# A fused spectral filter and gated FFN on one core: one weight load on another queue, and the first slabs' steps in another order

## The chip, the cores and the metric

The kernel runs on one core of one Trainium2 chip. The metric is the device time of one execution in microseconds; the time of a kernel is the median of its runs.

## What is computed

The input `x` is 2048 rows of 640 values. Each row is normalized; the normalized rows go two ways. One way is a spectral filter (a two-dimensional real Fourier transform, a product with complex weights, and the inverse transform), computed as matrix products with tables of sines. The other is a gated FFN with 1536 hidden columns. The two meet in the last line.

```python
xn = _layernorm(x, axis=-1)
s = irfft2(rfft2(xn) * (w_r + 1j * w_i)).astype(bfloat16)
h = gelu(xn @ w_gate) * (xn @ w_up)
g = silu(h @ w_down)
return x + s * g
```

## The kernel before

The rows are taken as 16 slabs of 128 rows (`n1` is the slab's number), and X holds them all in the on-chip memory. Four slabs make an FFN group of 512 rows. The hidden columns are 12 tiles of 128. For a group, each tile takes five products with the gate weights Wg (the 640 columns are five chunks of 128) and five with the up weights Wu. ScalarE turns the gate result into its gelu (tile `ge`, L805), and VectorE multiplies it by the up result into `uT` (L807). The products need the normalized rows transposed, `xnT`. For group 0 TensorE itself transposes, chunk by chunk, into a PSUM tile `pt`, and VectorE or ScalarE copies that to `xnT`. Later groups are transposed by DMA.

A slab is normalized in these steps: VectorE takes the statistics of two halves (`bn_half`, L180) and joins them (`bn_join`, L186); the reciprocal root is taken by ScalarE for slab 0 (`root_act`, L205) and by VectorE and GpSimd for the others (`root`: `ve` at L196, the power at L198); VectorE then subtracts and scales in place (`norm`, L209).

The order of all work is written out by hand. Each engine executes its instructions in the order in which the program names them, with semaphores for what it needs from others. `back` is the list of TensorE's FFN steps, and `put(s, ...)` places other work behind step `s`. The steps at the start are these:

- Before step 0: the loads (all on SP's queue), constants, statistics of slabs 0 and 1, warm-up products that feed nothing (`warm_pe`, L600), the normalization and transposes of slab 0 in two parts (`norm_parts`, `slab_Tparts`), the rest of slab 1's statistics and its root, and small constants (`inv_consts`, L261) on VectorE.
- Step 0: the gate products of tiles 0 and 1 for slab 0 (`GG`), slab 1's normalization, slab 0's up products of tile 0, slab 1's transposes, slab 0's up products of tile 1 (`UU`).
- Step 1: gate and up products of tiles 0 and 1 for slab 1; then slab 2's statistics.
- Steps 2 to 7: tiles 2 to 7 for the first half of the group (slabs 0 and 1, 256 columns). Behind them slab 2 is normalized (step 2) and transposed (step 4), slab 3 normalized (step 5) and transposed (step 6).
- Steps 8 to 15: tiles 0 to 7 for the second half (slabs 2 and 3). From step 16 on, tiles take 512 columns at once.

Weights come in pieces of two tiles (`load_w`, `load_gu`): each piece has 128 rows in five runs of 512 bytes, 320 KB. Slabs 0 to 3 are loaded one by one, 160 KB each, in rows of 1280 bytes.

The filter's stages lie between the later FFN steps and are not touched.

Of the kernel before, what the change touches and what calls it, by code (L numbers as in the profile page):

```python
# [32 lines left out]
def kernel(  # L33
# [40 lines left out]
    with tc.manual_schedule():  # L74
        build(nc, locals())


def build(nc, env):
    consts, big, wts, xg, work, psA, psB = (env[k] for k in ("consts", "big", "wts", "xg", "work", "psA", "psB"))
    ZDR, UDR, X, Wg, Wu, Wd, W1, W2 = (env[k] for k in ("ZDR", "UDR", "X", "Wg", "Wu", "Wd", "W1", "W2"))  # L80
    xv, outv, wgv, wuv = (env[k] for k in ("xv", "outv", "wgv", "wuv"))
    A_w_r, A_w_i, B_w_down = (env[k] for k in ("A_w_r", "A_w_i", "B_w_down"))

    def load_x(n0, n, eng=nc.sync):
        eng.dma_start(out=X[:, n0:n0 + n, :], in_=xv[:, n0:n0 + n, :])

    def load_w(k, t0, t1):
        f0, f1 = t0 * P, t1 * P
        nc.sync.dma_start(out=(Wg, Wu)[k][:, :, f0:f1], in_=(wgv, wuv)[k][:, :, f0:f1])

    def load_gu(t0, t1):
        for k in range(2):
            load_w(k, t0, t1)

    load_x(0, 1)
    load_x(1, 1)
    load_gu(0, 2)
    load_gu(2, 4)
    load_x(2, 1)
    load_gu(4, 6)  # L100
# [76 lines left out]
    def bn_half(n1, k):  # L177
        if k == 0:
            st_n[n1] = work.tile([P, 2, nc.vector.BN_STATS_DIM], FP32, tag="st", bufs=3, name="st")
        nc.vector.bn_stats(out=st_n[n1][:, k, :], in_=X[:, n1, 320 * k:320 * k + 320])  # L180

    def bn_join(n1):
        g = n1 // 4
        if g not in mva:
            mva[g] = work.tile([P, 4, nc.vector.BN_AGGR_DIM], FP32, tag="mva", bufs=2, name=f"mva{g}")
        nc.vector.bn_aggr(out=mva[g][:, n1 % 4, :], in_=st_n[n1])  # L186
# [6 lines left out]
    def root(n0, n):  # L193
        m = mva[n0 // 4][:, n0 % 4:n0 % 4 + n, :]
        ve = work.tile([P, 4], FP32, tag="ve", name="ve")[:, 0:n]
        nc.vector.tensor_scalar(out=ve, in0=m[:, :, 1], scalar1=1e-5, scalar2=None, op0=ALU.add)  # L196
        r = work.tile([P, 4], FP32, tag="rst", bufs=4, name="rst")[:, 0:n]
        nc.gpsimd.tensor_tensor(out=r, in0=ve, in1=mhalf[:, 0:n], op=ALU.pow)  # L198
        rall[n0] = r
        for k in range(n):  # L200
            rstd[n0 + k] = r[:, k:k + 1]
# [6 lines left out]
    def norm(n1, c0=0, c1_=D):  # L208
        nc.vector.tensor_scalar(out=X[:, n1, c0:c1_], in0=X[:, n1, c0:c1_], scalar1=mva[n1 // 4][:, n1 % 4, 0:1],  # L209
                                scalar2=rstd[n1], op0=ALU.subtract, op1=ALU.mult)  # L210
        if c1_ == D:
            done.add(("n", n1))
# [46 lines left out]
    def affine(name, src, a, b):  # L259
        t = c1(name)  # L260
        nc.vector.tensor_scalar(out=t, in0=src, scalar1=float(a), scalar2=float(b), op0=ALU.mult, op1=ALU.add)  # L261
        return t
# [43 lines left out]
    def inv_consts(part):  # L306
        if part == 0:
            for k, c in enumerate((0.0, 4.0, 2.0)):
                inv_src[k] = affine(f"i_{k}", pf, 4.0, c)
            kc.append(affine("hk", h_f, -2.0, 1.0))  # L310
        else:
            o = [affine(f"o_{k}", pf, 2.0, c) for k, c in enumerate((320.0, 2.0, 321.0, 1.0))]
            i_0, i_1, i_2 = (inv_src[k] for k in range(3))
            ab.extend([(i_0, o[0]), (i_1, o[1]), (i_2, o[2]), (i_2, o[3])])
# [281 lines left out]
    def warm_pe(n):  # L596
        if not warm_bank:
            warm_bank.append(bank(0))
        for _ in range(n):
            nc.tensor.matmul(warm_bank[0][:, 0:256], lhsT=ones[:, 0:P], rhs=ones, start=True, stop=True)  # L600
# [182 lines left out]
    def bank(k):  # L783
        return psA.tile([P, 512], FP32, tag="gu"[k], name="ps" + "gu"[k])
# [58 lines left out]
    GG, UU = ((0, 0), (1, 0)), ((0, 1), (1, 1))  # L843
# [2 lines left out]
        for it in items:  # L846
            it[0](*it[1:])

    PARTS = (((0, 3), (3, 5)), ((0, 2), (2, 5)))

    def norm_parts(n1):
        for a, b in PARTS[n1]:
            norm(n1, a * P, b * P)

    def slab_Tparts(n1):
        if n1 == 0:
            xnT[0] = xg.tile([P, 5, 512], BF16, tag="xg", name="xnT0")
        evs = (nc.scalar.copy, nc.vector.tensor_copy)
        for (a, b), ev in zip(PARTS[n1], evs[::-1] if n1 == 0 else evs):
            pt = psB.tile([P, 5, P], BF16, tag="b")  # L860
            for c in range(a, b):
                nc.tensor.transpose(out=pt[:, c, :], in_=X[:, n1, c * P:(c + 1) * P], identity=ident)
            ev(out=xnT[0][:, a:b, n1 * P:n1 * P + P], in_=pt[:, a:b, :])
        done.add(("T", n1))

    NP = 8
    back = [(run, (ffn_slab, 0, GG), (norm_parts, 1), (vt_iota, 1), (ffn_slab, 0, UU[:1]), (slab_Tparts, 1),
             (ffn_slab, 0, UU[1:])),
            (run, (ffn_slab, 1, GG + UU), (stats, 2), (root, 2, 1))]
    for h in range(2):  # L870
        for t in range(0 if h else 2, NP):
            back.append((ffn_part, 0, t, h))
    for g in range(4):
        for t in range(NP if g == 0 else 0, NT):
            for k in range(2):
                back.append((ffn_half, g, t, k))
        for j in range(4):
            for q in range(3):
                back.append((down_third, g, j, q))
    plan = [[] for _ in back]  # L880

    def put(s, *item):
        plan[s].append(item)
# [6 lines left out]
    put(4, root, 3, 1)  # L890
    put(4, slab_T, 2, 1)
    put(5, norm, 3)
    put(6, slab_T, 3, 0)
    for g in range(5):
        put(3 + g, ft_v, g)
        put(8 + g, ft_v, 5 + g)
# [79 lines left out]
    for i, (n0, n) in enumerate(DG):  # L976
        a = vs0 + 7 * i
# [12 lines left out]

    warm_pe(18)
    norm_parts(0)
    bn_half(1, 1)
    slab_Tparts(0)
    warm_pe(2)
    bn_join(1)
    root(1, 1)
    inv_consts(0)
    inv_consts(1)

    put(5, phase_const)

# [35 lines left out]
```

## Time and profile before

| | |
|---|---|
| median of 3 runs | 200.24 us (199.80 to 200.43) |
| profiled execution | 199.91 us, of which the profile's span is 198.0 us |
| TensorE busy | 192.3 us, 97% of the span |
| VectorE, ScalarE, GpSimd busy | 131.1, 124.0, 39.8 us |
| gate and up products (L801) | 60.5 and 60.6 us |
| down products (L826) | 30.5 and 28.9 us |
| moved by DMA | 32.43 MB, mean 164 GB/s |

Times in the profile are microseconds from the span's start. PE is TensorE (PEld its weight loads), DVE is VectorE, ACT is ScalarE, POOL is GpSimd, and SPq is the queue from which SP issues transfers. In a row of the timeline the first number is the start and the second the duration, then engine, source line and operation, output and input tiles, shape and count; a bracket gives the idle time ahead of it and what ended that. A row that stands for several instructions reaches from the start of the first to the end of the last, and ends of matmuls overlap the next start. The chain of waits is followed back from the last instruction to whatever released each step, and is listed here in order of time.

### The profile page before, as it was taken

How to read it: one execution, taken by the hardware profiler on the slowest of the kernel's cores; microseconds unless marked ns; L12 is line 12 of the kernel's file. 1: busy time of each engine (PE TensorE's matmuls, PEld its weight loads, DVE VectorE, ACT ScalarE, POOL GpSimd, SP SyncE). 2: the span in 40 equal slices, each digit the busy share in tenths (PEclk: the TensorE clock that was granted, in tenths of full speed). 3: DMA queues.
4: the chain of work that ended last, by engine and by line, in shares of the span. 5: the costliest groups of instructions: out<-in, count | busy, mean ns of one | idle time of the engine just before them, and what ended most of it. 6: DMA issues, size and time to landing. Idle time of an engine off the chain costs nothing.

```text
span 198.0 us, 4139 instructions
## 1 busy us (share of the span) xinstructions
PE 192.3 (97%) x1523; PEld 118.7 (60%) x1538; DVE 131.1 (66%) x314; ACT 124.0 (63%) x218; POOL 39.8 (20%) x68
## 2 busy tenths in 40 slices
PE   7999999999999999999999999999999999999993
PEld 5798854777555555676534343457765555556773
DVE  7787889979899831224666555333349786878673
ACT  4566657876976666634878687524474748376632
POOL 4448679997220110000000000000000000000000
PEclk9999999999999999999999999999999999999998
DMA  5999999657576783329962022439900416042612
GB/s 151 306 328 363 368 319 187 134 145 268 135 193 111 149 311 100 106 69 310 271 180 103 16 86 100 135 98 273 293 4 33 137 37 195 33 136 42 195 62 71
DMA packets 39508, 32.43 MB, mean 164 GB/s; under 512 B 13248, under 2 KB 38464, under 8 KB 39232
## 3 DMA queue, kind: packets, MB, share of 16 engines
q1 hardware_dynamic: 39392, 30.86, 55.4%
q0 software_dynamic: 96, 1.31, 1.7%
q8 instruction: 12, 0.20, 0.5%
q14 instruction: 8, 0.07, 0.1%
HBM read 19.03 MB, written 7.88 MB: 136 GB/s over the span
## 4 chain that ended last, share of the span: by engine, by line
PE 93%; DVE 3%; DMA 1%; issue 1%; ACT 1%; POOL 0%; ACTq 0%
PE psu L801 25%; PE psg L801 25%; PE psg L826 14%; PE psu L826 13%; PE pv L718 2%; PE pd L563 2%; PE pu L663 2%; PE pz L553 2%; PE pd L584 2%; PE px L636 2%; DMA X<-in_A_x_dram 1%; PE pd L567 1%; DVE st L180 1%; DVE X L209 1%; PE pd L586 1%
## 5 line engine op out<-in xcount | busy, mean ns | idle before, releaser
L801 PE MATMUL psg<-xnT,Wg 128*128 128x512 bf16 (+2 forms) x282 | 60.5, 341 | 0.7 <-issue 0.2
L801 PE MATMUL psu<-xnT,Wu 128*128 128x512 bf16 (+2 forms) x283 | 60.6, 342 | 0.4 <-issue 0.2
L807 DVE TENSOR_TENSOR uT<-psu,ge 128x512 bf16<-128x512 f32 (+2 forms) x58 | 34.4, 593 | 25.8 <-PE psu L801 22.9
L826 PEld LDWEIGHTS <-uT 128*128 128x128 bf16 x396 | 37.2, 98 | 14.1 <-issue 0.4
L805 ACT ACTIVATE ge<-psg 128x512 bf16<-128x512 f32 (+2 forms) x58 | 30.4, 523 | 23.1 <-PE psg L801 22.4
L801 PEld LDWEIGHTS <-Wu 128*128 128x128 bf16 x290 | 26.8, 98 | 23.8 <-issue 2.2
L801 PEld LDWEIGHTS <-Wg 128*128 128x128 bf16 x290 | 26.5, 98 | 20.8 <-issue 1.9
L826 PE MATMUL psg<-Wd,uT 128*128 128x320 bf16 (+1 forms) x204 | 30.5, 295 | 0.0
L826 PE MATMUL psu<-Wd,uT 128*128 128x320 bf16 (+1 forms) x192 | 28.9, 296 | 0.0
L648 DVE TENSOR_TENSOR X<-xs,W 128x972 bf16<-128x972 bf16 (+2 forms) x22 | 13.3, 648 | 10.2 <-ACT xs L644 9.2
L589 ACT CAST zd<-pd 128x660 bf16<-128x660 f32 x16 | 11.3, 706 | 10.0 <-PE pd L586 8.4
L180 DVE BATCH_NORM_STATS2 st<-X 128x6 f32<-128x320 bf16 x32 | 14.0, 475 | 0.3 <-DMA X<-in_A_x_dram 0.3
L720 ACT CAST W<-pv 128x640 bf16<-128x640 f32 x16 | 11.1, 696 | 5.0 <-PE pv L718 5.0
L743 ACT ACTIVATE W<-pd 128x960 bf16<-128x960 f32 (+2 forms) x14 | 10.1, 780 | 5.6 <-PE pd L567 5.5
L669 ACT CAST X<-pu 128x486 bf16<-128x486 f32 (+4 forms) x22 | 12.3, 558 | 0.3
L644 ACT CAST xs<-px 128x972 bf16<-128x972 f32 (+2 forms) x11 | 10.3, 937 | 2.9 <-PE px L636 2.9
L835 DVE SCALAR_TENSOR_TENSOR G<-th,psg 128x320 bf16<-128x320 f32 x8 | 3.9, 487 | 12.1 <-ACT th L834 12.1
L555 ACT CAST GEN<-pz 128x640 bf16<-128x640 f32 x16 | 11.2, 699 | 0.0
L749 DVE TENSOR_TENSOR W<-W 128x960 bf16<-128x960 bf16 (+1 forms) x12 | 6.9, 599 | 3.9 <-ACT W L743 3.8
L776 DVE TENSOR_TENSOR Yall<-Yall,G 128x640 bf16<-128x640 bf16 (+3 forms) x19 | 8.2, 434 | 1.6 <-ACT G L831 1.3
L777 DVE TENSOR_TENSOR Yall<-Yall,xt 128x640 bf16<-128x640 bf16 (+3 forms) x19 | 8.3, 439 | 0.7
L198 POOL TENSOR_TENSOR rst<-ve,mhalf 128x1 f32<-128x1 f32 (+1 forms) x6 | 5.4, 902 | 12.8 <-DVE ve L196 12.8
(144 smaller groups left out, 210.9 us busy)
## 6 DMA issues: line engine op xcount, KB each, us to landing
ZDR<-zd SPq DMA_DIRECT2D x32, 80.2 KB, 2.5
UDR<-X SPq DMA_DIRECT2D x10, 240.8 KB, 2.4
xt<-in_A_x_dram SPq DMA_DIRECT2D x14, 160.0 KB, 3.4
out_dram<-Yall SPq DMA_DIRECT2D x14, 160.0 KB, 1.9
B<-ZDR SPq DMA_DIRECT2D x8, 240.8 KB, 4.2
W<-UDR SPq DMA_DIRECT2D x4, 481.5 KB, 6.8
X<-in_A_x_dram SPq DMA_DIRECT2D x3, 640.0 KB, 10.2
Wd<-in_B_w_down_dram SPq DMA_DIRECT2D x1, 1920.0 KB, 14.6
```

The costliest lines, as they stand in the source:

```text
L180: nc.vector.bn_stats(out=st_n[n1][:, k, :], in_=X[:, n1, 320 * k:320 * k + 320])
L555: nc.scalar.copy(out=Zt[n1], in_=pz)
L589: nc.scalar.copy(out=zd.rearrange("p c (q e) -> p c q e", e=10), in_=pd[:, :, 0:330].rearrange("p c (e q) -> p c q e", q=33))
L644: nc.scalar.copy(out=xs, in_=px[:, :, 0:n * w].rearrange("p k (h l) -> p k h l", l=w))
L648: nc.vector.tensor_tensor(out=pp[-1], in0=xs, in1=WT[:, :, h0:h0 + n, l0:l0 + w], op=ALU.mult)
L669: nc.scalar.copy(out=us[:, :, :, c0:c0 + (w + 1 - m) // 2], in_=pv[:, :, :, m:w:2])
L720: nc.scalar.copy(out=vs, in_=pv)
L743: nc.scalar.activation(out=eo[:, b, :, a0:a1].rearrange("p k a n -> p a k n"), in_=py[b][:, a0:a1], func=ACT.Copy, scale=(2.0 if silu[a0] ...
L801: nc.tensor.matmul(ps, lhsT=WT[:, c, t * P:(t + 1) * P], rhs=xnT[g][:, c, c0:c1_], start=(c == 0), stop=(c == 4))
L805: nc.scalar.activation(out=ges[t], in_=ps, func=ACT.Gelu_apprx_tanh)
L807: nc.vector.tensor_tensor(out=uT[g][:, t, c0:c1_], in0=ps, in1=ges[t], op=ALU.mult)
L826: nc.tensor.matmul(ph, lhsT=uT[g][:, t, j * P:(j + 1) * P], rhs=Wd[:, t, c0:c1_], start=(t == 0), stop=(t == NT - 1))
```

## The change

The up weights of tiles 0 and 1 are issued from ScalarE's queue instead of SP's, as its first instruction. On VectorE, slab 1's join and root come ahead of the copy of slab 0's transposes. In step 0, slab 1's transposes come ahead of all of slab 0's up products. Slab 1 is split like slab 0 (three chunks, then two; VectorE copies the three and ScalarE the two). The second part of `inv_consts` moves behind slab 0's up products. Slab 3's transposes move from behind step 6 into step 7, between its gate and its up products, and are split in two parts as well. There is one warm-up product more behind slab 0's transposes.

```diff
-    def load_w(k, t0, t1):
+    def load_w(k, t0, t1, eng=nc.sync):
         f0, f1 = t0 * P, t1 * P
-        nc.sync.dma_start(out=(Wg, Wu)[k][:, :, f0:f1], in_=(wgv, wuv)[k][:, :, f0:f1])
+        eng.dma_start(out=(Wg, Wu)[k][:, :, f0:f1], in_=(wgv, wuv)[k][:, :, f0:f1])
...
     load_x(0, 1)
     load_x(1, 1)
-    load_gu(0, 2)
+    load_w(0, 0, 2)
+    load_w(1, 0, 2, nc.scalar)
     load_gu(2, 4)
...
-    PARTS = (((0, 3), (3, 5)), ((0, 2), (2, 5)))
+    PARTS = ((0, 3), (3, 5))
...
-        evs = (nc.scalar.copy, nc.vector.tensor_copy)
-        for (a, b), ev in zip(PARTS[n1], evs[::-1] if n1 == 0 else evs):
+        for (a, b), ev in zip(PARTS, (nc.vector.tensor_copy, nc.scalar.copy)):
...
-    back = [(run, (ffn_slab, 0, GG), (norm_parts, 1), (vt_iota, 1), (ffn_slab, 0, UU[:1]), (slab_Tparts, 1),
-             (ffn_slab, 0, UU[1:])),
+    back = [(run, (ffn_slab, 0, GG), (norm_parts, 1), (vt_iota, 1), (slab_Tparts, 1), (ffn_slab, 0, UU),
+             (inv_consts, 1)),
...
+        if h == 0:
+            back[-1] = (run, (ffn_piece, 0, NP - 1, 0, 0, 256), (slab_Tparts, 3), (ffn_piece, 0, NP - 1, 1, 0, 256))
...
-    put(6, slab_T, 3, 0)
...
     warm_pe(18)
     norm_parts(0)
     bn_half(1, 1)
-    slab_Tparts(0)
-    warm_pe(2)
     bn_join(1)
     root(1, 1)
+    slab_Tparts(0)
+    warm_pe(3)
     inv_consts(0)
-    inv_consts(1)
```

## The prediction

> **What bounds the kernel now.** I read the page first, then the chain that ended last in order of time, then the timeline and the rates of the first 20 us, where the edits lie.
>
> The chain's shares by engine, on the page:
>
> ```profile
> PE 93%; DVE 3%; DMA 1%; issue 1%; ACT 1%; POOL 0%; ACTq 0%
> ```
>
> TensorE sets the end. Read in order of time, the chain leaves TensorE only in the first 16 us and in the last one; between, it holds nothing but matmuls and gaps of 0.02 to 0.16 us. So a product that starts 0.1 us earlier at 9 or 16 us moves the end by 0.1 us, and nothing later absorbs it. The chain around slab 1:
>
> ```profile
> 5.28 0.40 DVE st L180
> 5.68 0.30 DVE xnT L863
> 5.98 0.13 DVE mva L186
> ...
> 6.13 0.17 DVE ve L196
> ...
> 6.37 0.59 POOL rst L198
> ...
> 6.98 0.36 DVE X L209
> ...
> 7.39 0.29 PE pt L862 x2
> ...
> 8.05 0.37 DVE xnT L863
> ...
> 8.46 0.61 PE psg L801 x8
> 9.07 0.56 PE psu L801 x10
> ```
>
> The copy of slab 0 (5.68) stands inside slab 1's way from statistics to transposes, and TensorE takes up slab 1's gate products fully only at 8.46. The last row gives 0.056 us for a 128-column product. The second place is slab 3, in the timeline:
>
> ```profile
> 14.66 0.71 PE L801 MATMUL psu<-xnT,Wu 128*128 128x256 bf16 x5
> 14.95 0.43 DVE L209 TENSOR_SCALAR X<-X,mva,rst 128x640 bf16<-128x640 bf16 x1
> ...
> 15.44 0.28 PEld L541 LDWEIGHTS <-X 128*128 128x128 bf16 x5 [0.36 <-DVE X L209]
> 15.45 0.45 PE L541 MATMUL pt<-ident,X 128*128 128x128 bf16 x5
> ```
>
> A group of five 256-column products takes 0.54 (the next rows start 0.54 or 0.55 apart), so TensorE was free at 15.20 and began the transposes at 15.45: 0.25 us lost to slab 3's normalization, done at 15.38.
>
> The loads at the start, in the same view:
>
> ```profile
> 0.72 1.28 ACT L221 ACT_TABLE_LOAD   x1 [0.72 <-PEq L1022]
> 0.72 0.86 SPq L85 DMA_DIRECT2D X<-in_A_x_dram  x2
> ...
> 1.64 0.43 SPq L89 DMA_DIRECT2D Wg<-in_B_w_gate_dram  x1
> ...
> 2.10 0.53 SPq L89 DMA_DIRECT2D Wu<-in_B_w_up_dram  x1
> ...
> 4.32 0.29 ACT L205 ACTIVATE rst<-mva,eps 128x1 f32<-128x1 f32 x1 [2.10 <-DVE mva L186]
> ```
>
> The chain begins with slab 0's load, 0.72 to 3.13. Today nothing else moves beside it but slab 1.
>
> **Slab 1 ahead.** Without the copy, the aggregation starts at 5.68 + 0.02. Its whole length is 0.21 (0.08 of that ran under the copy), then 0.02, ve 0.17, 0.07, the power on GpSimd 0.59, 0.03: slab 1's normalization starts at 6.79, not 6.98, a gain of 0.19. The copy (0.36) follows ve, 6.02 to 6.38, and the four inv_consts(0) instructions (0.33 in all) end about 6.65; both lie under the power on GpSimd. The price is slab 0's gate products: their first starts at 6.42 instead of 6.04, ten end at 6.98, before the transposes can start. Today ScalarE's half of that copy ends at 6.38 anyway, so only about 0.1 us of it would show, and TensorE idles then. The third warm-up product (0.11 to 0.21) lies in the same idle time.
>
> The normalization now takes 384 columns first: 0.38 (slab 0's row: 0.64 for both parts, as here), plus 0.05, so three transposes start at 7.22; the other two at 6.79 + 0.64 + 0.05 = 7.48. The ten up products of slab 0 start at 7.59 and end at 8.15. VectorE's copy is ready at 7.22 + 0.36 + 0.37 = 7.95, ScalarE's (0.32 after 7.48, plus 0.37) at 8.17, wanted by the fourth gate product at 8.32. So slab 1's gate runs 8.15 to 8.71 without a stop, and its up products start at 8.71 against 8.91: **0.20 us gained**. The five up products that today fill TensorE's wait ahead of the transposes come behind them; that takes back most of what the wait loses, and is why the gain is not larger. The four inv_consts(1) instructions (0.33) move behind slab 0's up products on VectorE, queued ahead of slab 1's; there VectorE idled 0.76 before 9.46. Cost nothing; were that cover gone, at most 0.33 on VectorE, which TensorE would see only at slab 2's transposes (normalization done 12.38, wanted 12.63).
>
> **Slab 3 in tile 7.** The transposes come one gate group later, at 15.74 on today's clock, 0.36 after the normalization ends. The stall of 0.25 goes: **0.25 us gained**. What is late next are the copies, which keep one up group (0.54) as cover instead of two. VectorE: three transposes from 15.74, copy from 16.12 (behind tile 6's product, 15.47 to 15.89) to 16.48, wanted at 16.57. ScalarE: gelu of tile 7 from 15.94 to 16.32, copy to 16.67, wanted by the fourth product at 16.90. Margins 0.09 and 0.23; a miss costs itself, at most the 0.25.
>
> **The up load from ScalarE's queue.** Its issue (0.53, from SP's row) goes ahead of the table load and warm-up; these then end near 2.75, and ScalarE idled 2.10 before 4.32. Nothing, unless the issue exceeded 2.1 us. On SP every later issue moves up by up to 0.57. The real cost is at the DMA engines:
>
> ```profile
> 2.00:3.00 1.00, 1.00 (x6) 0.74 (x5) 0.77 (x11) 0.20 (x2) 0.13 (x1) 1.00 0.80 285
> 3.00:4.00 1.00, 1.00 (x7) 0.69 (x6) 0.85 (x2) 0.00 (x0) 0.89 (x1) 1.00 0.61 174
> ...
> 5.00:6.00 1.00, 1.00 (x8) 0.74 (x8) 1.00 (x5) 0.99 (x2) 0.00 (x0) 1.00 1.10 314
> ```
>
> (The last two columns are DMA share and GB/s.) The up load now leaves at 0.72 beside slab 0. Its 328 KB at 300 GB/s are 1.09 us, slab 0's 164 KB are 0.55. If all of it goes first, slab 0 is 1.09 late; with equal shares, 0.55; if slab 0's bytes are on the engines first, 0. No row shows two such queues together. I take 0.25, the nearer half: the smaller load also has the shorter issue (0.43 against 0.53), so it should reach the engines no later. The whole chain from 3.13 shifts by that: **0.25 us lost**. The dip at 3 to 4 us (some 0.12 MB) is filled, so the loads behind come up to 0.4 us earlier; this matters only as cover: the up weights of tiles 6 and 7 land at 8.43 + 6.0 = 14.4 and are wanted at 14.55, a margin that the earlier TensorE would else eat. Slab 1's load (1.17 + 2.4 = 3.57) has until 4.20; 0.63 of delay is free.
>
> The Trainium skill, "DMA: Bandwidth & Descriptors", section "Queues, rings and completion order", speaks against this edit: each engine takes turns between queues by packets of about 9 to 17 descriptors. An estimate from it: one such packet of 512-byte rows on 16 engines is 74 to 139 KB, or 0.25 to 0.46 us ahead of slab 0; by its upper end the sum below would be 0.01 above the time before.
>
> **Sum.** -0.20 - 0.25 + 0.25 = -0.20 us. The profiled execution took 199.91 (span 198.0 and 1.91 around it), which is 0.33 below the median 200.24; it becomes 199.71, and the median 200.04.
>
> **Rivals.**
> 1. Slab 0's load is not held at all: -0.45, 199.79. For it: its issue is first on SP and short. Against: both queues start at 0.72.
> 2. Slower: the up load holds slab 0. It decides from 0.45 us of delay on; with equal shares the time is 200.34, with all of its bytes first 200.88. For it: the chain starts with that load and has no slack. Against: slab 0's rows are few, and equal turns by row favour it (1280 bytes against 512). The skill's turns by packets, above, would stop it at 0.46 us of delay and 200.25.
> 3. The TensorE clock rises later. The warm-up shows 4.02 us for 18 products of 256 columns, 0.22 each, and later groups 0.11: in the records the rate doubles between slab 0's transposes (0.107 apart) and its gate products (0.055 apart), near 5.7. The granted-clock column reads 1.00 throughout and does not show it. If it doubled only after slab 1, products at 0.107 put slab 1's up products at 9.86 in the old order and 10.16 in the new one, which has 25 products and transposes between slab 1's normalization and that point where the old has 20. Then +0.30 in place of -0.20, in all 200.54. The new kernel's later start gives TensorE a slightly longer pause before it, which speaks a little for it. The skill's "TensorE: Matmul & The Clock Gate", section "What's actually happening", says the window that decides runs freely, not from the kernel's start; by that the moment varies between executions of either kernel.
> 4. The change does less than it says: the copies of slab 3 miss their cover and the 0.25 comes back: 200.29.
>
> **Chances.** Forecast 0.52, rival 1 0.20, rival 2 0.17, rival 3 0.07, rival 4 0.04. A measurement of this kernel can tell about 0.3%, 0.60 us, from no change (the three runs spread over 0.63). The sum's best case is 0.45, so faster by more needs something that I don't see as well: 0.12, from rival 1. Slower by more needs nearly the whole up load ahead of slab 0, or rivals 2 and 3 together: 0.14. The range runs from rival 1 with half of the runs' spread (199.79 - 0.3) to rival 2's far end: 199.5 to 200.88.
>
> **What would show it.** Slab 0's load in the chain: landing by 3.13 + 0.25 (3.13: rival 1; 3.7 or later: rival 2). Relative to that landing, slab 1's normalization should start 3.66 after it (3.85 today) and its up products 5.58 (5.78 today). The wait of 0.36 at slab 3's transposes should be gone, and tile 0's second half should follow tile 7's up group without a gap. I am wrong if the statistics of slab 0 start on time and the time still doesn't fall, if slab 0's gate products wait for weights beyond 6.98 plus the shift, or if a new wait stands after 17 us.

## The result and the profile after

The changed kernel takes 201.16 us in the median of 22 runs (200.29 to 202.99), the kernel before 199.97 us in as many (199.80 to 201.10). The ratio is 1.0049, 95% interval 1.0031 to 1.0067: slower by half a per cent, above the range of the prediction.

The 22 runs fall into two groups. Ten lie between 200.29 and 200.66 us, twelve between 201.11 and 202.99. So there are two losses: about 0.5 us that every execution has, and one of 0.65 us or more that about half of them have. The profiled execution (202.09 us) has both. Its page begins with the span (198.0 before); part 3 shows the up load as a queue of its own:

```profile
span 200.3 us, 4157 instructions
...
q10 hardware_dynamic: 656, 0.33, 0.6%
```

The chain of waits in order of time (start, duration, what):

```profile
1.17 4.10 DMA X<-in_A_x_dram
...
5.30 0.49 DVE st L181
5.79 0.53 DVE X L210 x2
...
7.24 0.59 POOL rst L199
...
7.86 0.39 DVE X L210
...
8.29 0.69 PE pt L862 x5
8.98 1.07 PE psu L802 x10
10.05 1.07 PE psg L802 x10
```

The chain no longer begins with slab 0's load but with slab 1's. That load, issued at 1.17, landed at 5.27; before, 2.4 after its issue, near 3.55. VectorE takes slab 1's first statistics ahead of slab 0's normalization, so the normalization, 4.65 before, starts at 5.71 in the timeline. ScalarE's root for slab 0 had ended at 5.21, 0.60 later than before (4.61), so of the 1.06 us slab 0's own late landing makes 0.60 and the wait for slab 1 the other 0.46. The second thing to see is the length of the last two rows: ten products of 128 columns take 1.07, where before they took 0.56.

The reason stands in the table by stage (columns: stretch, its length, busy time of TensorE, its weight loads, VectorE, ScalarE, GpSimd, then granted clock, DMA share, GB/s):

```profile
4.95:8.36 3.41, 1.84 (x21) 1.20 (x20) 2.80 (x13) 2.51 (x6) 0.58 (x1) 1.00 1.13 295
8.36:11.77 3.41, 3.41 (x34) 3.37 (x35) 1.33 (x10) 1.08 (x4) 1.57 (x4) 0.50 1.15 304
```

The granted clock is one half from 8.36 to 11.77, a stretch of 3.41 us. The trace's clock record begins at 4.95 with full speed. Ahead of its first entry the column reads 1.00 too, although the products run at half speed there, as the prediction noted under its third rival. In the 3.41 us before the fall TensorE was busy for 1.84; it had paused twice, as the brackets show:

```profile
6.13 0.54 PE L862 MATMUL pt<-ident,X 128*128 128x128 bf16 x5 [0.99 <-DVE X L210]
7.48 0.72 PE L802 MATMUL psg<-xnT,Wg 128*128 128x128 bf16 x10 [0.48 <-DVE xnT L863]
```

The Trainium skill, "TensorE: Matmul & The Clock Gate", section "What's actually happening", gives a window of that length (3413 ns) for the decision, and the trace agrees with the length. It also speaks of an idle window as what lets the clock fall; here a window that was 54% busy was enough, and the measurement decides.

The mean granted clock of each execution shows that this second fall is not the whole of the second loss. Of the twelve slower executions six, the profiled one among them, have 0.988 to 0.992 (201.56 to 202.99 us). The other six (201.11 to 201.94 us) have 1.000, as all ten of the lower group have: their clock did not fall again. A first rise that comes late would not show in this figure; none of these six was traced.

Where the first loss comes from is seen in the rows of the DMA queues from the start to 3.7 us (packets, MB, share of the engines' time):

```profile
q10 hardware_dynamic: 507, 0.26, 23.8%
q1 hardware_dynamic: 144, 0.16, 19.6%
```

By then 507 of the up piece's 640 rows had moved, 32 for each of the 16 engines. SP's queue (q1) had moved slab 0's 128 rows and 16 small packets, and nothing of slab 1, which had been issued at 1.17. Slab 0 had lagged even before that: by 2.7 us, when the first rows of the up piece start to move, SP's queue had 75 packets through, against 180 in the kernel before. The part at slab 3 did what it was to do; TensorE's timeline around tile 7:

```profile
17.62 0.71 PE L802 MATMUL psg<-xnT,Wg 128*128 128x256 bf16 x5
18.17 0.44 PE L862 MATMUL pt<-ident,X 128*128 128x128 bf16 x5
18.45 0.71 PE L802 MATMUL psu<-xnT,Wu 128*128 128x256 bf16 x5
18.99 0.71 PE L802 MATMUL psg<-xnT,Wg 128*128 128x256 bf16 x5
```

The transposes start 0.55 after the gate products, without a wait, and tile 0's second half starts 0.54 after the up products, so the two copies were in time.

### The profile page after: what moved, and what is told of

Same layout as the page of the kernel before. It is cut to its first block, busy times and chain, and to the rows that moved or that the text cites. A ratio compares the mean times of both kernels' runs of the same rounds, so it can differ in the third digit from the quotient of the medians.

```text
span 200.3 us, 4157 instructions
## 1 busy us (share of the span) xinstructions
PE 194.2 (97%) x1539; PEld 120.1 (60%) x1539; DVE 131.1 (65%) x314; ACT 124.4 (62%) x219; POOL 39.8 (20%) x68
## 4 chain that ended last, share of the span: by engine, by line
PE 94%; DMA 2%; DVE 1%; POOL 0%; issue 0%; SPq 0%; ACT 0%
PE psu L802 27%; PE psg L802 26%; PE psg L827 14%; PE psu L827 13%; PE pv L719 2%; PE pd L564 2%; PE pu L664 2%; PE pz L554 2%; DMA X<-in_A_x_dram 2%; PE pd L585 2%; PE px L637 2%; PE pd L568 1%; PE pd L587 1%; PE pt L862 0%; DVE X L210 0%; DVE st L181 0%
## 5 line engine op out<-in xcount | busy, mean ns | idle before, releaser
L802 PE MATMUL psg<-xnT,Wg 128*128 128x512 bf16 (+2 forms) x290 | 61.7, 346 | 0.5 <-DVE xnT L863 0.5
L802 PE MATMUL psu<-xnT,Wu 128*128 128x512 bf16 (+2 forms) x290 | 62.1, 348 | 0.0
L802 PEld LDWEIGHTS <-Wu 128*128 128x128 bf16 x290 | 27.7, 101 | 23.7 <-issue 2.2
```

The source lines that it names most:

```text
L802: nc.tensor.matmul(ps, lhsT=WT[:, c, t * P:(t + 1) * P], rhs=xnT[g][:, c, c0:c1_], start=(c == 0), stop=(c == 4))
```

## The experiments

Each kernel ran beside the kernel before on the same chip; its median was 199.85 to 200.03 us in the five comparisons.

### One part at a time

**All but the up load.** The changed kernel with the load back on SP:

```diff
-    load_w(0, 0, 2)
-    load_w(1, 0, 2, nc.scalar)
+    load_gu(0, 2)
```

> The changed kernel with the up weights of tiles 0 and 1 back on SP's queue; all else changed. Theory A (the up load on the second queue holds slabs 0 and 1, 1.06 us at slab 0's normalization; the longer pause of TensorE then lets its clock fall for 3.41 us in part of the executions): both losses go, and the two gains of the prediction are left, -0.45 us against the kernel before, near 199.45; normalization of slab 0 at 4.65, of slab 1 at 6.79, slab 1's up products at 8.71, no second stretch at half clock. Rival B (the new order of slab 1 and the later copies cost the time, the load's queue is harmless): as slow as the changed kernel, 200.4 to 201.2.

Measured: ratio 0.9995 (0.9979 to 1.0012); ten executions lie between 199.28 and 200.74 us. Two more, at 0.56 and 0.66 of the clock, took 335.7 and 287.8 us; the profiled one is the first of these and can't be read beside the others, so the same kernel was run again.

> The same kernel as the one with all but the up load changed, run once more for a profile that can be compared with the others. Theory A with the loads as second limit (with the up piece back on SP, the up weights of tiles 4 to 7 land as late as before the change while TensorE comes to them 0.2 us earlier, and some executions wait for them): -0.2 to 0 us against the kernel before in the median, the best executions at -0.45, and waits of the up products of tiles 4 or 6 for their weights in the profile. Rival (the clock rises later in this kernel): no such waits, but products 0.107 apart beyond 7 us.

Measured: 199.52 us, ratio 0.9987 (0.9972 to 1.0002), from 199.24 to 201.11. The loss of the changed kernel is gone, which is against rival B. The best executions are 0.5 us faster than the best of the kernel before (199.71), as the sum of both gains says, but both intervals still include 1, since the executions spread. The waits for weights that were expected are not in the profiled one (199.24 us, span 197.5), and neither are products at half speed beyond 7 us. TensorE's timeline has both steps where the prediction put them:

```profile
8.60 0.72 PE L801 MATMUL psu<-xnT,Wu 128*128 128x128 bf16 x10
...
14.90 0.71 PE L801 MATMUL psg<-xnT,Wg 128*128 128x256 bf16 x5
15.44 0.44 PE L861 MATMUL pt<-ident,X 128*128 128x128 bf16 x5
15.72 0.71 PE L801 MATMUL psu<-xnT,Wu 128*128 128x256 bf16 x5
```

Slab 1's up products start at 8.60, with slab 0 landed at 3.0; 8.71 was forecast for a landing at 3.13.

**The up load alone**, in the kernel before:

```diff
...
-    load_gu(0, 2)
+    load_w(0, 0, 2)
+    load_w(1, 0, 2, nc.scalar)
```

> The kernel before with only the up load moved to ScalarE's queue. Theory A: slab 1's load lands near 5.27 instead of 3.55, slab 0's normalization starts near 5.7 instead of 4.65, and the time is +1.06 us (200.9) where the clock stays up, and 1 to 2 us more where it falls a second time. Rival B: no change, within 0.2 us of the kernel before.

Measured: 200.73 us, ratio 1.0050 (1.0029 to 1.0070); five of eight executions lie between 200.63 and 200.74, the other three between 201.27 and 202.07, all at a granted clock of 0.999 or more. Its chain:

```profile
1.17 3.90 DMA X<-in_A_x_dram
...
5.09 0.49 DVE st L181
5.58 0.54 DVE X L210 x2
```

Slab 1 lands at 5.07 and the normalization starts at 5.58, 0.93 late. The price is 0.8 to 0.9 us, a little under the 1.06 expected, and the second fall of the clock that was expected in part of the executions did not come. By the ratios (1.0050 and 1.0049) the load by itself costs as much as the whole change.

**Tile 7 alone**, in the kernel before:

```diff
...
+        if h == 0:
+            back[-1] = (run, (ffn_piece, 0, NP - 1, 0, 0, 256), (slab3_T,), (ffn_piece, 0, NP - 1, 1, 0, 256))
...
-    put(6, slab_T, 3, 0)
```

> The kernel before with only slab 3's transposes moved into tile 7 and split in two parts. Theory A and the prediction's step: -0.25 us (199.65 if the kernel before is at 199.9), the wait of 0.36 us of weight loads for slab 3's normalization gone. Rival B (the copies miss their cover of one up group): 0 to -0.1, with a new wait at the first product of the second half.

(`slab3_T` makes slab 3's transposes and copies in two parts, as the changed kernel does.) Measured: 199.54 us, ratio 0.9981 (0.9971 to 0.9991), within 199.43 and 199.84. The step of the prediction (-0.25) stands; -0.33 was measured.

**The order of slab 1 alone**: the changed kernel with the up load on SP and slab 3's transposes back behind step 6.

```diff
-    load_w(0, 0, 2)
-    load_w(1, 0, 2, nc.scalar)
+    load_gu(0, 2)
...
-        if h == 0:
-            back[-1] = (run, (ffn_piece, 0, NP - 1, 0, 0, 256), (slab_Tparts, 3), (ffn_piece, 0, NP - 1, 1, 0, 256))
...
+    put(6, slab_T, 3, 0)
```

> The kernel before with only the order of slab 1 changed (join and root ahead of the copy, transposes ahead of the up products, third warm-up product, second part of the constants later). Theory A and the prediction's step: -0.20 us, slab 1's up products at 8.71 instead of 8.91. Rival B: slower by 0.1 to 0.5, since 25 instead of 20 products stand between slab 1's normalization and its up products and the clock may rise later.

Measured: 200.20 us, ratio 1.0012 (0.9995 to 1.0029), spread over 199.59 to 201.31. The list of waits between 11 and 16.5 us of its profiled execution (200.61 us) names one that the kernel before does not have:

```profile
PEld L801 <- DMA Wu<-in_B_w_up_dram: 1.4, 2, 0.9
```

TensorE waited for the up weights of tiles 4 and 6, which landed at 12.23 and 15.51; in the kernel before they landed at 11.76 and 14.41, just ahead of need. The interval includes 1, so a loss by the order is not shown; the gain that was expected did not come.

### The clock

**Longer warm-up** in the changed kernel:

```diff
-    warm_pe(18)
+    warm_pe(24)
...
-    warm_pe(3)
+    warm_pe(8)
```

> The changed kernel with 24 instead of 18 warm-up products ahead of slab 0's transposes and 8 instead of 3 behind them, so that TensorE hardly pauses between 5.0 and 7.5. Theory A2 (the pauses let the clock fall again for 3.41 us in part of the executions): no second stretch at half clock, the executions gather near 200.4, and the median falls from 201.16 to 200.4 to 200.6; the 0.5 us of the late loads stay. Rival (the clock's moments have nothing to do with the pauses): executions spread as for the changed kernel, 200.3 to 203.

Measured: 200.43 us, ratio 1.0024 (1.0013 to 1.0036); all nine executions lie between 200.36 and 200.67. The upper group is gone: the median is 0.58 us above the kernel before instead of 1.19. So TensorE's pauses make that group; both numbers of warm-up products were changed at once, and which of them it takes was not tested. The chain shows the same late load, and full speed behind it:

```profile
1.18 3.90 DMA X<-in_A_x_dram
...
8.65 0.56 PE psu L802 x10
```

**Shorter warm-up** in the kernel before, with no load held:

```diff
-    warm_pe(18)
+    warm_pe(12)
```

> The kernel before with 12 instead of 18 warm-up products: nothing else is changed, no load is held, but TensorE pauses from about 3.7 to 5.1 instead of hardly at all. Theory A2 (pauses at the start let the clock rise later or fall again): part of the executions are 0.5 to 2 us slower than the kernel before, the median is up by 0.2 us or more. Rival (the pause alone does nothing; only together with held loads or the new order): no change, within 0.1 us.

Measured: 200.75 us, ratio 1.0038 (1.0017 to 1.0058), with executions up to 202.04. The mean granted clock is 1.000 in all twelve, so it fell in none. What came later in the profiled one is the first rise: its clock record begins at 8.28, that of the kernel before at 5.69. In its chain ten products take 1.17 us ahead of that moment and 0.56 behind it:

```profile
6.08 1.17 PE psg L801 x10
...
9.43 0.56 PE psu L801 x10
```

So a pause of TensorE costs time by itself, without a held load and without a fall of the clock.

### Size and moment of the load on the second queue

**Slab 1 on ScalarE's queue too, ahead of the up piece:**

```diff
-    load_x(1, 1)
+    load_x(1, 1, nc.scalar)
```

> The changed kernel with slab 1's load also on ScalarE's queue, ahead of the up load, while SP issues slab 0. Theory A: slab 1 (8 rows per engine) is ahead of the up load's 40 rows and lands by 3.7; slab 0 lands between 3.1 and 3.7; slab 0's normalization starts 0 to 0.5 later than in the kernel before instead of 1.06, and the time is -0.45 to 0 us against it. Rival (the loss comes from slab 0's late landing, not slab 1's): slab 0 lands near 3.73 as in the changed kernel, normalization near 5.25, +0.15 us.

Measured: 200.45 us, ratio 1.0032 (1.0016 to 1.0048). Slab 1 landed at 3.96, but slab 0 at 3.77 instead of 3.1, and the statistics of slab 0 started 0.64 late. The rows are the rival's (normalization at 5.28, 5.25 expected), but the time is outside what either expected. A second queue that starts at the same moment delays slab 0 as well, even with as few rows as slab 0 has itself.

**One chunk of five from ScalarE's queue:**

```diff
-    load_w(1, 0, 2, nc.scalar)
+    nc.scalar.dma_start(out=Wu[:, 0:1, 0:256], in_=wuv[:, 0:1, 0:256])
+    nc.sync.dma_start(out=Wu[:, 1:5, 0:256], in_=wuv[:, 1:5, 0:256])
```

> The changed kernel with one of the five chunks of that up piece on ScalarE's queue at the start (8 rows per engine instead of 40) and the four others on SP behind the gate piece. Theory A (an engine finishes the other queue's transfer before it turns back to slab 1): slab 1's load is held by a fifth, 0.2 to 0.3 instead of 1.72, less than the 0.63 it has to spare; what is left is slab 0's own lateness, 0 to 0.6; time -0.45 to +0.15 us. Rival (opening a second queue at all delays slab 1): slab 1 still lands after 4.5 and the time is +0.4 or more.

Measured: slab 1 landed at 3.79, 0.24 late, and slab 0 at 3.29. So slab 1's lateness goes with the rows of the other queue's transfer: 40 per engine 1.72 (1.52 and 1.53 in two other traces), 8 per engine 0.24. The time, 200.68 us, ratio 1.0037 (1.0016 to 1.0059), is a miss that this does not explain; the executions spread from 199.92 to 202.19, as in the order alone.

**Behind the table load**, in the changed kernel:

```diff
-    load_w(1, 0, 2, nc.scalar)
...
     nc.scalar.activation(out=warm, in_=eps, func=ACT.Abs_reciprocal_sqrt)
+    load_w(1, 0, 2, nc.scalar)
```

ScalarE's queue issued it at 1.19, while the table load (0.72 to 2.00) still ran.

> The changed kernel with the up load still on ScalarE's queue, but issued behind the table load and the first activation, near 2.2 us, when the packets of slabs 0 and 1 are nearly through. Theory A (slab 1's load waits for the up load's turn on the engines): slab 1 lands near 3.6 as before the change, slab 0's normalization starts at 4.65, both gains stay: -0.3 to -0.5 us against the kernel before. Rival (a second queue as such slows the loads, or the order costs the time): 200.2 or more.

Measured: 199.61 us, ratio 0.9984 (0.9974 to 0.9994), ten of eleven executions between 199.49 and 199.80. Slab 0 lands at 3.10, slab 1 at 4.28, right at the need. The gain, 0.24 us, is a little short of the 0.3 to 0.5 expected: the gate piece, now behind the up piece, lands at 6.53 instead of 5.71, and slab 0's gate products wait for it (start 6.57). Still, that 0.5 us of delay turns the changed kernel from 0.5% slower into 0.16% faster.

The same place of the load with only the order of slab 1 (slab 3's transposes back behind step 6, as above), and with only tile 7 (in the kernel before, as above):

> The new order of slab 1 with the up load on ScalarE's queue behind the table load, and slab 3's transposes where they were before the change. If the order alone (+0.33 us in the median before) lost its gain to weights that land late, it shows here, since those weights come 0.3 us earlier: -0.1 us, executions close together. If the order itself costs time (more products behind slab 1's normalization), it is slower again by 0.1 to 0.4.

> The kernel before with slab 3's transposes in tile 7 and the up load on ScalarE's queue behind the table load, slab 1 in the old order. Theory A: slab 1's load lands near 4.3, just at the need, the weights behind it 0.3 us earlier: -0.25 to -0.35 us, as with tile 7 alone (-0.33), executions close together. If a second queue costs as such: -0.1 or worse.

Measured: 199.67 us, ratio 0.9986 (0.9977 to 0.9995), for the order; 199.69 us, ratio 0.9990 (0.9982 to 0.9999), for tile 7, where slab 1 landed at 4.42 and held the normalization by about 0.2. Tile 7 gains 0.16 here, less than expected (0.25 to 0.35). With weights that come earlier (tile 6's at 13.89) the order gains 0.18; with the load on SP its median had been 0.33 above the kernel before, not clear of noise.

**Later still**, in the changed kernel. First at the place behind the table load, behind an activation that reads slab 0 (issued at 3.10); then at its old place, behind one that writes a column of the load's destination (issued at 2.25):

```diff
+    nc.scalar.activation(out=warm, in_=X[:, 0, 0:1], func=ACT.Abs_reciprocal_sqrt, bias=eps)
     load_w(1, 0, 2, nc.scalar)
```

```diff
+    one = consts.tile([P, 1], FP32, name="one")
+    nc.vector.memset(one, 1.0)
+    nc.scalar.activation(out=Wu[:, 0, 0:1], in_=one, func=ACT.Abs_reciprocal_sqrt)
     load_w(1, 0, 2, nc.scalar)
```

> The changed kernel with the up load on ScalarE's queue behind a small activation that reads slab 0, so that it is issued near 3.2 us. Theory A: slab 0 lands at 3.1 and slab 1 at 3.55 as in the kernel before, the gate piece before 6.4, the up piece near 7.3: both gains whole, -0.45 us (199.4). If the order's gain is lost in any case, -0.25.

> The changed kernel with the up load on ScalarE's queue at its old place in the program, but behind a small activation that first writes one column of the load's destination, so that it is issued near 2.25 (the attempt before it held ScalarE until 6.88, because the load came after all the others in the program and waited for the second gate piece). Slab 1 lands by 3.8, the up piece near 6.5, the up weights of tiles 4 to 7 about 0.3 us earlier than in the kernel before. If the spread of the kernel with the load back on SP and the loss of the order alone come from weights that land late, both gains are whole, -0.45 us (199.4), with the executions within 0.5 us of each other. If they come from the order itself: above 199.5, spread over 1 us.

Measured: 203.37 us, ratio 1.0138 (1.0104 to 1.0172), and 200.54 us, ratio 1.0018 (0.9993 to 1.0043). Slabs 0 and 1 were on time in both (3.0 and 3.5), but now the up piece came late: it shares the engines with the gate pieces that SP had issued before it, and landed at 9.93 and 8.11, where it is wanted near 7.5. In the second, the profiled execution (200.91 us) has tile 0's second half only 0.12 later than the kernel before (16.95 against 16.83); the rest of its loss lies behind that and was not followed up. The up load in the chain of the first, and its table by stage:

```profile
3.10 6.83 DMA Wu<-in_B_w_up_dram
```

```profile
9.00:10.00 1.00, 0.02 (x1) 0.03 (x2) 0.00 (x0) 0.00 (x0) 0.00 (x0) 1.00 1.17 297
10.00:11.00 1.00, 1.00 (x14) 1.00 (x15) 0.32 (x2) 0.00 (x0) 0.00 (x0) 0.71 1.13 299
```

TensorE's weight loads wait 2.5 us, and half a us after it starts again the clock falls to one half, here with another cause of the pause.

Set beside the traces above, these landings show what decides which load waits. The up piece landed behind slab 0 and ahead of slab 1 when it was issued at 0.72 (slab 1: 1.17), behind slab 1 and ahead of SP's gate piece when it was issued at 1.19 (gate piece: 1.64), and behind two gate pieces and the next up piece of SP's queue when it was issued at 3.10. In no trace did one of these loads overtake another that had been issued more than 0.2 us earlier, on whichever queue. As far as these traces go, the moment of issue decided, not the queue.

A third, with the load behind an activation that reads `e64` among the constants, failed in another way:

```diff
+    nc.scalar.activation(out=warm, in_=e64, func=ACT.Abs_reciprocal_sqrt, bias=eps)
+    load_w(1, 0, 2, nc.scalar)
     hi1 = affine("hi1", hi_f, -1536.0, 1536.0)
```

> The changed kernel with the up load on ScalarE's queue behind a small activation that reads a constant which VectorE finishes near 2.0 us, so that it is issued near 2.05. Its first bytes should come near 3.0, when those of slabs 0 and 1 are through: slab 1 lands by 3.7, the up piece near 6. If the spread of the kernel with the load back on SP (199.24 to 201.11) and the loss of the order alone come from weights that land late, then here both gains are whole, -0.45 us (199.4), and the executions lie within 0.4 us of each other. If they come from the order itself, the median stays above 199.5 with a spread of over 1 us.

Measured: 208.00 us, ratio 1.033 (1.0279 to 1.0381). The load stood in the program behind all the others and was issued only at 6.88, when the second gate piece had landed (6.86); ScalarE's queue holds its instructions in order, so slab 0's root waited too:

```profile
7.36 0.29 ACT L205 ACTIVATE rst<-mva,eps 128x1 f32<-128x1 f32 x1 [4.82 <-DMA Wg<-in_B_w_gate_dram]
```

## Why the prediction was wrong

**The bound** was right: in the changed kernel nothing behind tile 0's second half took up or added time. From its start to the end of the span it is 181.2 us before (198.0 - 16.83) and 181.3 after. In the other kernels here this rest was 181.2 to 181.7, and 182.2 in the one with the load at 2.25 (the one at 0.56 of the clock left aside); what makes that difference was not followed up.

**Slab 1 ahead** was right in its steps. Slab 1's normalization was to start 6.79 + 1.06 = 7.85 with the shift, and started at 7.86; the transposes were to start at 8.28 and did so at 8.29. It brings about 0.2 us if its cover holds. The cover was named (up weights of tiles 6 and 7, margin 0.14), but its price was not put into the range: with the load on SP, one profiled execution lost 1.1 us there and another nothing. That the spread of the two such kernels comes from this alone is not shown.

**Slab 3 in tile 7** was right: 0.25 forecast, 0.33 measured alone.

**The up load from ScalarE's queue** is the step that failed, in two places. The term was 0.25 us; it is 1.06 in the changed kernel. First, slab 0 landed 0.60 late (3.73), by the prediction's own mark rival 2, with equal shares; the reason given for the nearer half, the shorter issue, did not count. That is 0.60 of the 1.06. Second, "Slab 1's load has until 4.20; 0.63 of delay is free": that load was treated as cover, while it stood behind the whole up piece and landed 1.72 late. This put at nothing the other 0.46: slab 1, not slab 0, set the start in the end. The far end of the range priced slab 0 behind all 40 rows per engine, 1.09; nobody priced slab 1 there.

The rule weighed at that place (the Trainium skill, "DMA: Bandwidth & Descriptors", "Queues, rings and completion order": turns of 9 to 17 descriptors) gave 0.25 to 0.46. That section calls 9 to 17 typical and 64 the ceiling; the prediction used the typical ones alone. The rows speak against turns that short here: 507 rows of the up piece, 32 per engine, before the first of slab 1, which lies under the ceiling. They also show a delay that goes with the size of the whole transfer. That the piece of 40 rows per engine is one such turn is not shown; the traces do not tell the engines apart.

**The clock** was a rival at 0.07, priced at 0.30 for a late rise. TensorE's pauses, which the late load brings about (0.99 and 0.48 us in the profiled execution), decided the median: with more warm-up products in their place the upper group is gone. In six executions the clock fell a second time, which the prediction had not considered. In the other six of that group it did not fall, and the rival as it was stated, a late rise, is left as the likely cause: it is what the shorter warm-up shows (first rise at 8.28, granted clock 1.000). For these six it is argued and not shown. Rivals 2 and 3 were taken as separate cases with one small chance for both together; here the first is the cause of the second. That is why the far end, 200.88, was too low: 1.06 - 0.45 = 0.6 puts the lower group at 200.5, which was measured (200.29 to 200.66), and the upper group lies above that.

Four kernels are faster than the kernel before by 0.10 to 0.19 per cent, with intervals wholly below 1: tile 7 alone (0.9981), the changed kernel with the load behind the table load (0.9984), and the two that have half of that each (0.9986 and 0.9990).

## What to carry to other kernels

A load that is moved to a second queue is not added beside the first queue's loads but put among them: list every load that is under way in those microseconds, with the time of its issue and the time at which it is wanted, and price each of them behind the whole of what is issued ahead of it, on either queue. Where the start of a kernel hangs on one small load, give that load and the next one the engines first; here 0.5 us later for the weights was worth some 1.4 us of the median. And a stall of TensorE near the start can cost more than its length, since in part of the executions the clock falls again behind it, or first rises later; products that feed nothing are a cheap test of it, and here they took that loss away.

## What the runs showed that was not expected

- A transfer of 40 rows per engine on the other queue held the next load of SP's queue for 1.52 to 1.72 us, one of 8 rows for 0.24.
- Slab 0's load landed at 2.98 to 3.14 whenever the second queue was silent before 1.1 us, and at 3.29 to 3.77 whenever a load was issued there at 0.72, be it with 8 rows per engine or 40.
- The clock fell for one stretch of 3.41 us (three in a row in the kernel at 208 us) behind windows in which TensorE was busy for 1.84, 1.09 and 0.46 of 3.41 us, and stayed up behind 1.86 and more. All traces but the one at 0.56 of the clock were read in such windows, forward and back from the first entry of the clock record. They fit two limits: the clock was lost behind 1.84 (the changed kernel) and less and kept behind 1.86 (slab 1 on ScalarE's queue, the rows below) and more; it rose behind 2.79 (the same kernel) and more and not behind 2.73 (the kernel at 208 us) and less. The shorter warm-up had 2.47 in the window that ends at 4.87, and its clock rose one window later. Where such windows begin differs from execution to execution (the first rise lies between 3.96 and 8.28 us in these traces), which fits a loss that only part of the executions have.

```profile
3.96:7.37 3.41, 1.86 (x20) 1.27 (x19) 3.19 (x14) 2.04 (x4) 0.53 (x1) 1.00 1.17 300
7.37:10.78 3.41, 3.31 (x51) 2.98 (x49) 2.65 (x13) 1.57 (x6) 1.61 (x5) 1.00 1.14 303
```

- ScalarE's queue issued a load at 1.19 while its table load ran until 2.00.
